# Attention with row sums in the output matmul: output blocks 130 PSUM columns apart in place of 129

## The chip, the cores and the metric

The kernel runs on one NeuronCore of a Trainium2 chip. The metric is device time in microseconds (us), from executions of the whole program. A time is the median of several runs. A profile is one more execution with every instruction recorded. On one core a run's state is "fast" unless it is over 1.5% above the fastest of its kernel.

## The reference, cut to what matters

```python
B, H, Sq, Sk, D = 16, 32, 192, 1024, 128          # bf16
scores = einsum("bhqd,bhkd->bhqk", q, k) * D ** -0.5
p = softmax(scores, axis=-1)
out = einsum("bhqk,bhkd->bhqd", p, v)
```

There are 512 heads, and the kernel takes them two at a time: 256 pairs of heads.

## The kernel before: the parts that matter here

For each head TensorE transposes the keys (`tr`), multiplies keys by queries (`qk`), and multiplies exponentials by values (`pv`). ScalarE computes the exponentials, VectorE copies the transposed keys to SBUF and normalises the output, POOL copies the values into rows that end in a one. That extra column makes the output matmul 129 columns wide: column 128 of the result is the row sum.

The 192 queries are three blocks j of 64. The two heads x of a pair use the two column halves of the array. So one key tile t of one block j is a *couple* of matmuls (x = 0 and 1) that run together, and a pair of heads needs 3 x 8 = 24 couples, issued as two halves of 12.

```python
VB = 130
vp = sb("f_vp", [128, R, 2 * T, VB], BF16)          # value rows: 128 values, ones; 260 bytes apart
o_ps = ps("f_o", [128, 512], F32)                   # one PSUM bank for the output of a pair
# ... TensorE:
order = [(j, t) for j in range(3) for t in range(T)]    # T = 8 key tiles

def pv(p, lo, hi):
    if lo == 0:
        take(s_vp, 1)
        # ...
        if 1 <= p <= NPR - 3:
            take(s_on, 1)                           # VectorE has read the pair before out of o_ps
    O = o_of(p)
    for j, t in order[lo:hi]:
        for x in range(2):
            ins = pe.matmul(
                O[64 * x: 64 * x + 64, j * 129: j * 129 + 129],
                pt[:, (2 * p + x) % NP, t * SQ + j * 64: t * SQ + j * 64 + 64],   # stationary
                vp[:, p % R, x * T + t, 0:129],                                   # moving
                start=t == 0, stop=t == T - 1, skip_group_check=True,
                tile_position=(0, 64 * x))
    # ...

def step(n):
    for x in range(2):
        h = 2 * n + x
        qk(h); tr(h + 2); pv(n - 2, 12 * x, 12 * x + 12)     # bounds left out
# steps run in a hardware loop of R = 4 steps per iteration
# ... VectorE, once a pair:
def onorm(p):
    O = o_of(p)[:, 0:387].rearrange("p (j c) -> p j c", j=3)
    ri = rinv[:, 3 * p: 3 * p + 3]
    dve.wait_ge(s_pv, p + 1)
    dve.reciprocal(ri, O[:, :, 128]).then_inc(s_rc, 1)
    dve.wait_ge(s_rc, p + 1)
    # ...
    dve.tensor_tensor(ob[:, so, a, :].rearrange("p (j d) -> p j d", j=3), O[:, :, 0:128],
                      ri.unsqueeze(2).to_broadcast([128, 3, D]), ALU.mult,
    ).then_inc(s_on if p < NPR - 1 else s_fin, 1)
```

Of the kernel before, what the change touches and what calls it, by code (L numbers as in the profile page):

```python
# [26 lines left out]
def _general_path(nc, q, k, v, out, redo, G=16, NS=2, LAGS=(2, 4, 5, 7), ROUTES=(R_W, R_W, R_EA)):  # L27
# [46 lines left out]
    with ExitStack() as es:  # L74
# [137 lines left out]
        def _(pe):  # L212
# [48 lines left out]
            def pv(u):  # L261
# [5 lines left out]
                if k3 == 0 and pr >= 2:  # L267
                    pe.wait_ge(s_on, pr - 1)
                O = o_ps[pr % 2]
                PTS = pt_sb[:, u % NPT]  # L270
# [5 lines left out]
                for t in range(KT_TILES):  # L276
                    first = t == 0
                    last = t == KT_TILES - 1
                    if k3 < 2:
                        x = a if k3 == 0 else b  # L280
                        ins = pe.matmul(O[:, sl, :], PTS[:, t, :], vs[:, s, x, t, :],
                                        start=first, stop=last, skip_group_check=True)
                        if with_rs:
                            ins = pe.matmul(O[:, 3, sl: sl + 1], PTS[:, t, :], ones[:, 0:1],
                                            start=False, stop=last, skip_group_check=True)
                    else:
                        pe.matmul(O[0:64, sl, :], PTS[:, t, 0:64], vs[:, s, a, t, :],
                                  start=first, stop=last, skip_group_check=True, tile_position=(0, 0))
                        ins = pe.matmul(O[64:128, sl, :], PTS[:, t, 64:128], vs[:, s, b, t, :],
                                        start=first, stop=last, skip_group_check=True, tile_position=(0, 64))  # L290
                        if with_rs:
                            pe.matmul(O[0:64, 3, sl: sl + 1], PTS[:, t, 0:64], ones[:, 0:1],
                                      start=False, stop=last, skip_group_check=True, tile_position=(0, 0))
# [108 lines left out]
def _attention_kernel(nc, q, k, v, out, NVS=6):  # L402
# [12 lines left out]
    VB = 130  # L415
# [10 lines left out]
    with ExitStack() as outer:  # L426
# [23 lines left out]
        with ExitStack() as es:  # L450
# [25 lines left out]
            def o_of(p):  # L476

                if p == NPR - 1:
                    return s_ps[0][:, 0:512]
                if p == NPR - 2:  # L480
                    return k_ps[:].bitcast(F32)
                return o_ps[:]
# [88 lines left out]
            def _(pe):  # L571

                def take(s, c):
                    pe.wait_ge(s, c).then_inc(s, -c)  # L574
# [42 lines left out]
# [3 lines that stand above are left out]
                        if p == NPR - 1:  # L620
                            take(s_exp, 2)
                        if 1 <= p <= NPR - 3:
                            take(s_on, 1)
                    O = o_of(p)
                    ins = None
                    for j, t in order[lo:hi]:
                        for x in range(2):
                            ins = pe.matmul(  # L628
                                O[64 * x: 64 * x + 64, j * 129: j * 129 + 129],
                                pt[:, (2 * p + x) % NP, t * SQ + j * 64: t * SQ + j * 64 + 64],  # L630
                                vp[:, p % R, x * T + t, 0:129],
                                start=t == 0, stop=t == T - 1, skip_group_check=True,
                                tile_position=(0, 64 * x))
                    if hi == len(order):
                        ins.then_inc(s_pv, 1)
# [4 lines that stand above are left out]
                        if h < NH:  # L640
                            qk(h)
                        if h + 2 < NH:
                            tr(h + 2)
                        if n >= 2:
                            pv(n - 2, 12 * x, 12 * x + 12)
# [22 lines left out]
            @block.vector  # L668
            def _(dve):
                def evac(h):  # L670
                    p, x = divmod(h, 2)
                    dve.wait_ge(s_tr, h + 1)
                    if p >= R:
                        dve.wait_ge(s_qk, h - 2 * R + 1)
                    dve.tensor_copy(  # L675
                        kt[:, p % R, 8 * x: 8 * x + 8, :],
                        k_ps[:].rearrange("d (t c) -> d t c", c=128),
                    ).then_inc(s_ev, 1)

                where = {}  # L680
                for i, (p0, c) in enumerate(stores):
                    for a in range(c):
                        where[p0 + a] = (i, a)

                def onorm(p):
                    i, a = where[p]
                    so = i % NSO
                    O = o_of(p)[:, 0:387].rearrange("p (j c) -> p j c", j=3)
                    ri = rinv[:, 3 * p: 3 * p + 3]
                    dve.wait_ge(s_pv, p + 1)  # L690
                    dve.reciprocal(ri, O[:, :, 128]).then_inc(s_rc, 1)  # L691
                    dve.wait_ge(s_rc, p + 1)
                    if a == 0 and i >= NSO:
                        dve.wait_ge(s_st[so], 16 * (i // NSO))
                    dve.tensor_tensor(  # L695
                        ob[:, so, a, :].rearrange("p (j d) -> p j d", j=3),
                        O[:, :, 0:128],
                        ri.unsqueeze(2).to_broadcast([128, 3, D]),
                        ALU.mult,
                    ).then_inc(s_on if p < NPR - 1 else s_fin, 1)  # L700

                cnt = [0]

                def check(lo, hi, i, part):
                    c = chk[:, lo:hi]
                    if part == 0:
                        ins = dve.tensor_scalar(c, rinv[:, lo:hi], 1.0 / RS_HI, 1.0 / RS_LO, ALU.max, ALU.min)  # L707
                    elif part == 1:
                        ins = dve.tensor_tensor(c, c, rinv[:, lo:hi], ALU.not_equal)  # L709
                    else:  # L710
                        ins = dve.tensor_reduce(bad[:, i: i + 1], c, mybir.AxisListType.X, ALU.max)  # L711
                    ins.then_inc(s_dv, 1)
                    cnt[0] += 1
                    dve.wait_ge(s_dv, cnt[0])

                evac(0)
                evac(1)
                for n in range(NPR + 2):
                    for x in range(2):
                        h = 2 * n + 2 + x  # L720
                        if h < NH:
                            evac(h)
                    if n >= 2:
                        onorm(n - 2)
                        if 0 <= n - 2 - EARLY < 3:
                            check(0, 3 * EARLY, 0, n - 2 - EARLY)
                for part in range(3):
                    check(3 * EARLY, 3 * NPR, 1, part)
                dve.sem_inc(s_fl, 1)  # L729
                dve.wait_ge(s_fl, 2)  # L730
                dve.tensor_copy(redo[0:1, 0:1], o_ps[0:1, 0:1]).then_inc(s_fl, 1)  # L731
                dve.wait_ge(s_fl, 3)
# [48 lines left out]
```

## Time and profile before

| | before |
|---|---|
| median of the first 3 runs | 978.72 us (978.32 to 980.33) |
| span of the profiled run, granted clock | 975.8 us, 0.994 |
| one pair of heads in the steady part (mean, from the trace's start times) | 3670.5 ns; times 256: 939.6 us |

These are lines of the page of the kernel before: the busy time of each engine with its share of the span, and three rows of the costliest groups. A group's row has line, engine, operation, output and inputs, shape, count; then busy us and mean ns of one; then the engine's idle time just before them.

```profile
PE 949.3 (97%) x30730; PEld 943.4 (97%) x30730; DVE 546.5 (56%) x1031; ACT 743.8 (76%) x513; POOL 267.5 (27%) x263
...
L628 PE MATMUL f_o<-f_vp,f_pt 128*64 128x129 bf16 x12192 | 455.1, 221 | 0.3 <-PEq L574 0.3
...
L695 DVE TENSOR_TENSOR f_ob<-f_o,f_rinv 128x384 bf16<-128x384 f32 x254 | 141.6, 558 | 9.0 <-DVE f_rinv L691 0.3
L691 DVE RECIPROCAL f_rinv<-f_o 128x3 f32<-128x3 f32 x254 | 46.0, 181 | 5.0 <-PE f_o L628 2.4
```

TensorE is the busy engine and the others have room. The view of waits says who waited for whom; here are its longest lines and TensorE's longest (total us, times, longest us).

```profile
POOL f_vp L565 <- PE f_o L628: 671.7, 251, 5.9
DVE f_kt L675 <- PE f_k L588: 404.2, 509, 6.1
ACT f_pt L740 <- PE f_s L609: 220.7, 509, 5.8
...
PE f_s L609 <- issue: 6.4, 4, 3.1
```

Everyone waits for TensorE and TensorE seems to wait for nobody. That isn't quite so. The Trainium skill, "Perfetto Trace Analysis", section "Tensor Engine Instruction (MATMUL, LD_WEIGHTS)", says that a matmul's recorded end is an estimate, while its start is a recorded event. So start times were compared. This is the timeline of one pair (start us, duration us, engine, line, operation, count):

```profile
401.87 0.90 PE L628 MATMUL f_o<-f_vp,f_pt 128*64 128x129 bf16 x24
...
402.57 0.86 PE L609 MATMUL f_s<-f_qt,f_kt 128*64 128x192 bf16 x20
402.80 0.18 DVE L691 RECIPROCAL f_rinv<-f_o 128x3 f32<-128x3 f32 x1
...
403.02 0.56 DVE L695 TENSOR_TENSOR f_ob<-f_o,f_rinv 128x384 bf16<-128x384 f32 x1
...
403.24 0.64 PE L588 MATMUL f_k<-f_ident,f_kn 128*64 128x128 bf16 x16
...
403.72 0.89 PE L628 MATMUL f_o<-f_vp,f_pt 128*64 128x129 bf16 x24
```

The second half of a pair's output matmuls starts at 401.87 and the next group at 402.57. Reciprocal and multiply follow and end at 403.58, and the next pair's output starts at 403.72. The transposes at 403.24 would have let it start about 0.03 us earlier, at 403.69. A gap that short hides under matmul records of 0.22 us, so the table of waits doesn't show it.

### The profile page before, as it was taken

The page shows a single profiled execution, that of the slowest core. Times are in us where ns is not written, and L with a number is a line of the kernel's source. Part 1 is how long each engine was busy: PE and PEld are TensorE (multiplying, and loading weights), DVE is VectorE, ACT ScalarE, POOL GpSimd, SP SyncE. Part 2 cuts the span into 40 slices and gives each one's busy share as a digit, 9 for nine tenths or more (in the row PEclk, how much of TensorE's full clock was granted, in tenths as well). Part 3 has the DMA queues.
Part 4 walks back from the last instruction along what each step waited for, and adds up shares of the span by engine and source line. Part 5 has one row for each costly group of instructions (what it writes and reads, how often), then busy time and mean ns, then how long its engine had stood idle before and what let it go on. Part 6 is the DMA issues. An engine that isn't in the chain of part 4 may idle for free. (4 is left out here: it accounts for less than half of the span.)

```text
span 975.8 us, 67645 instructions
## 1 busy us (share of the span) xinstructions
PE 949.3 (97%) x30730; PEld 943.4 (97%) x30730; DVE 546.5 (56%) x1031; ACT 743.8 (76%) x513; POOL 267.5 (27%) x263
## 2 busy tenths in 40 slices
PE   5899999999999999999999999999999999999996
PEld 4799999999999999999999999999999999999985
DVE  2355655555555555555556555555555555565563
ACT  4577777777777777777777777777777777777774
POOL 2222222222222222222222222222222222222220
PEclk9899999999999999999999999999999999999999
DMA  9899999999999999999999999999999999999991
GB/s 263 237 331 347 346 330 345 343 324 351 346 323 350 345 334 342 331 343 341 349 329 341 331 348 335 344 337 319 365 336 336 348 338 330 349 337 327 352 321 44
DMA packets 279631, 319.32 MB, mean 327 GB/s; under 512 B 115744, under 2 KB 148512, under 8 KB 279584
## 3 DMA queue, kind: packets, MB, share of 16 engines
q1 hardware_dynamic: 279584, 318.84, 103.1%
q14 instruction: 35, 0.29, 0.1%
q8 instruction: 12, 0.20, 0.1%
HBM read 268.44 MB, written 25.17 MB: 301 GB/s over the span
## 5 line engine op out<-in xcount | busy, mean ns | idle before, releaser
L740 ACT ACTIVATE f_pt<-f_s 128x1536 bf16<-128x1536 f32 x512 | 742.5, 1450 | 220.8 <-PE f_s L609 220.7
L675 DVE COPY f_kt<-f_k 128x1024 bf16<-128x1024 bf16 x512 | 354.1, 692 | 407.0 <-PE f_k L588 404.2
L565 POOL COPY f_vp<-f_vs 128x1024 uint32<-128x1024 uint32 x256 | 266.7, 1042 | 690.4 <-PE f_o L628 671.7
L628 PE MATMUL f_o<-f_vp,f_pt 128*64 128x129 bf16 x12192 | 455.1, 221 | 0.3 <-PEq L574 0.3
L609 PE MATMUL f_s<-f_qt,f_kt 128*64 128x192 bf16 (+2 forms) x10240 | 443.3, 231 | 10.9 <-issue 6.4
L628 PEld LDWEIGHTS f_o<-f_vp,f_pt 128*64 128x64 bf16 x12192 | 391.7, 110 | 0.6 <-issue 0.6
L609 PEld LDWEIGHTS f_s<-f_qt,f_kt 128*64 128x64 bf16 x10240 | 359.2, 110 | 11.9 <-issue 11.8
L588 PE MATMUL f_k<-f_ident,f_kn 128*64 128x128 bf16 x8192 | 329.2, 219 | 6.2 <-PEq L574 4.8
L588 PEld LDWEIGHTS f_k<-f_ident,f_kn 128*64 128x64 bf16 x8192 | 286.1, 110 | 8.8 <-issue 8.6
L695 DVE TENSOR_TENSOR f_ob<-f_o,f_rinv 128x384 bf16<-128x384 f32 x254 | 141.6, 558 | 9.0 <-DVE f_rinv L691 0.3
L691 DVE RECIPROCAL f_rinv<-f_o 128x3 f32<-128x3 f32 x254 | 46.0, 181 | 5.0 <-PE f_o L628 2.4
L650 PE MATMUL f_o<-f_ones 128*128 128x512 bf16 x8 | 3.6, 631 | 1.1 <-POOL f_ones L555 1.1
L650 PEld LDWEIGHTS f_o<-f_ones 128*128 128x128 bf16 x8 | 1.0, 141 | 2.7 <-issue 1.7
L740 ACT ACT_TABLE_LOAD x1 | 1.3, 1283 | 0.8 <-PEq L766 0.8
L628 PE MATMUL f_s<-f_vp,f_pt 128*64 128x129 bf16 x48 | 1.8, 220 | 0.1
L628 PEld LDWEIGHTS f_s<-f_vp,f_pt 128*64 128x64 bf16 x48 | 1.5, 110 | 0.2 <-issue 0.2
L665 PEld LDWEIGHTS f_o<-f_bad,f_ones 128*1 128x1 bf16 x1 | 0.1, 79 | 1.6 <-DVEq L729 1.6
L628 PE MATMUL f_k<-f_vp,f_pt 128*64 128x129 bf16 x48 | 1.6, 220 | 0.0
L665 PE MATMUL f_o<-f_bad,f_ones 128*1 128x1 bf16 x1 | 0.2, 164 | 1.4 <-DVEq L729 1.4
L628 PEld LDWEIGHTS f_k<-f_vp,f_pt 128*64 128x64 bf16 x48 | 1.5, 110 | 0.0
L709 DVE TENSOR_TENSOR f_chk<-f_chk,f_rinv 128x744 f32<-128x744 f32 (+1 forms) x2 | 1.4, 706 | 0.0
L711 DVE TENSOR_REDUCE f_bad<-f_chk 128x1 bf16<-128x744 f32 (+1 forms) x2 | 1.1, 550 | 0.0
(15 smaller groups left out, 4.0 us busy)
## 6 DMA issues: line engine op xcount, KB each, us to landing
f_vs<-in_v_dram SPq DMA_DIRECT2D x256, 512.0 KB, 4.9
f_kn<-in_k_dram SPq DMA_DIRECT2D x255, 512.0 KB, 5.8
out_dram<-f_ob SPq DMA_DIRECT2D x63, 384.0 KB, 5.0
f_qt<-in_q_dram SPq DMA_TRANSPOSE x256, 4.6
f_kn<-in_k_dram SPq DMA_DIRECT2D x2, 256.0 KB, 2.9
out_dram<-f_ob SPq DMA_DIRECT2D x1, 288.0 KB, 2.3
out_dram<-f_ob SPq DMA_DIRECT2D x1, 96.0 KB, 2.0
```

Source lines behind the costliest of these rows:

```text
L565: gp.tensor_copy(vp[:, p % R, :, 0:D].bitcast(U32), vs[:, p % NVS, :, :].rearrange("p x (t d) -> p (x t) d", d=D).bitcast(U32),).then_inc( ...
L588: ins = pe.transpose(k_ps[64 * z: 64 * z + 64, t * 128: t * 128 + 128], kn[:, p % R, x, c0: c0 + 64], ident[:], tile_position=(0, 64 * z))
L609: ins = pe.matmul(S[64 * w: 64 * w + 64, c0: c0 + (j1 - j0) * 64], kt[:, p % R, 8 * x + t, 64 * w: 64 * w + 64], mv, start=True, stop=True ...
L628: ins = pe.matmul(O[64 * x: 64 * x + 64, j * 129: j * 129 + 129], pt[:, (2 * p + x) % NP, t * SQ + j * 64: t * SQ + j * 64 + 64], vp[:, p ...
L650: pe.matmul(o_ps[:], ones[:], ones[:].unsqueeze(1).to_broadcast([128, 4, 128]), start=True, stop=True)
L665: pe.matmul(o_ps[0:1, 0:1], ones[:, 0:1], bad[:, 0:1], start=True, stop=False)
L675: dve.tensor_copy(kt[:, p % R, 8 * x: 8 * x + 8, :], k_ps[:].rearrange("d (t c) -> d t c", c=128),).then_inc(s_ev, 1)
L691: dve.reciprocal(ri, O[:, :, 128]).then_inc(s_rc, 1)
L695: dve.tensor_tensor(ob[:, so, a, :].rearrange("p (j d) -> p j d", j=3), O[:, :, 0:128], ri.unsqueeze(2).to_broadcast([128, 3, D]), ALU.mul ...
L709: ins = dve.tensor_tensor(c, c, rinv[:, lo:hi], ALU.not_equal)
L711: ins = dve.tensor_reduce(bad[:, i: i + 1], c, mybir.AxisListType.X, ALU.max)
L740: act.activation(pt[:, h % NP, :], s_ps[h % 2][:], ACT_FN.Exp, scale=scale).then_inc(s_exp, 1)
```

## The change

A PSUM column is 4 bytes here. Blocks at columns 0, 129, 258 begin at bytes 0, 516 and 1032: the middle one is not at a multiple of 8. At 0, 130, 260 all are. The Trainium skill, "PSUM — Partial Sum Buffer", Specifications, gives PSUM 8-byte cachelines, and the presumable intent was to start each block on such a line. No instruction, wait or byte is added or removed; the instruction streams of both kernels are otherwise the same.

```diff
-                                O[64 * x: 64 * x + 64, j * 129: j * 129 + 129],
+                                O[64 * x: 64 * x + 64, j * VB: j * VB + 129],
...
-                    O = o_of(p)[:, 0:387].rearrange("p (j c) -> p j c", j=3)
+                    O = o_of(p)[:, 0:3 * VB].rearrange("p (j c) -> p j c", j=3)
```

## The prediction

> **What bounds the kernel now.** The page's busy table has TensorE at 97% of the span of 975.8 us, ScalarE 76%, VectorE 56%, POOL 27%; the clock was 0.994. The table of waits has almost nothing on TensorE's side (under 20 us), while ScalarE waits 221 us and VectorE 404 us for it. From the start times of single matmuls in the trace (steady part), one pair of heads takes 3670.5 ns: two score blocks of 668, two transpose blocks of 447 and 473, two output blocks (12 pairs of matmuls each) of 702 and 713. 256 pairs make 939.6 us; the rest is start and end.
>
> **What the change touches.** Blocks j=0,1,2 of the output stood at columns 0, 129, 258, so at bytes 0, 516, 1032; now 0, 130, 260, so at bytes 0, 520, 1040. Only j=1 began off an 8-byte boundary. The Trainium skill, "PSUM — Partial Sum Buffer", Specifications, gives PSUM 8-byte cachelines; the presumable intent is to have every block start on one, for TensorE's writes and VectorE's reads. No instruction, wait, byte or column is added or removed.
>
> **TensorE's share.** Before already holds the comparison, since j=0 and j=2 are aligned and j=1 is not. Median distances between successive pairs of matmuls, for four key tiles: j=0 56, 59, 59, 59; j=1 56, 60, 59, 59 (first half) and 57, 61, 59, 59 (just after the transposes); j=2 56, 60, 59, 59. The misaligned block is no slower: its means for four are 234.5 and 236.1 against 235.0 (j=0) and 234.0 (j=2). Even if the whole 2 ns were alignment it would be about 0.5 us (estimate: 2 ns x 256). The 3 ns that three of four pairs pay follows the key tile, not j: it goes with the moving operand's rows, 260 bytes apart, which the change leaves alone.
>
> **VectorE's share.** The one consumer is the pair of reciprocal (181 ns) and multiply (558 ns, 384 elements; groups by form), and it is on the critical path: the first matmul of the next pair's output comes 148 ns after the multiply's end in practically every pair, 1179 ns after the last matmul of the previous one. In about three of four pairs this holds TensorE 34 ns beyond its usual 26 (in the others the loop's end delays TensorE by about 40 anyway). So a faster multiply would be worth up to 34 ns x 192 = 6.5 us, and a slower one costs fully. But I expect no change: three runs of 128 elements, none merged with the next in either layout; at most one more line touched in one run of three, about 1 ns of 558, so 0 to 0.3 us.
>
> **Predicted time.** 978.72 - 0.3 = 978.4 us, range 975.5 to 981.0 (runs of before alone spread over 2 us). Chances: faster by over 2% 0.01, within 2% 0.98, slower 0.01.
>
> **What would show it.** Right: the output matmuls' mean stays at 220 to 221 ns and the distances of j=1 as above; the multiply stays at 557 to 559 ns and reciprocal at 181; output blocks stay at 702 and 713 and the first output matmul stays 148 ns behind the multiply. Wrong: the multiply falls by 10 ns or more with the 60 ns gap before the output's first matmul shrinking; or the j=1 distances change; or the pattern over key tiles (56, 59, 59, 59) changes with the output's place.
>
> **What would make it wrong.** A penalty of misaligned PSUM rows hidden in VectorE's 558 ns, which I can't separate (before has no aligned variant of the multiply); or a write penalty that is spread over neighbouring blocks because the matmuls are pipelined, so that j=1's cost appears under all three. Both would make it faster, by under 1%. Slower I see only through an access that the wider stride makes dearer for VectorE.

## More of the kernel before

The output matmuls' mean of 221 ns is the length of one record; records overlap, so it isn't their rate. The group's busy time, 455.1 us, is the union of the records, and does follow the rate.

## The result, and the profile after

| | before | after |
|---|---|---|
| median us, same rounds (lowest to highest, 4 runs each) | 979.36 (978.32 to 980.33) | 978.27 (977.1 to 980.2) |
| ratio after / before | | 0.9996, 95% interval 0.998 to 1.0011 |
| profiled span us, granted clock | 975.8, 0.994 | 977.0, 0.992 |
| one pair, steady part, ns | 3670.5 | 3668.6 |

The ratio and its interval are from fast runs of the same rounds; the ratio is not the quotient of the medians quoted (0.9989), which lies in the interval too. The time is the same. The lines of the page of the kernel after that answer to those above:

```profile
PE 951.1 (97%) x30730; PEld 945.5 (97%) x30730; DVE 546.7 (56%) x1031; ACT 744.3 (76%) x513; POOL 268.5 (27%) x263
...
L628 PE MATMUL f_o<-f_vp,f_pt 128*64 128x129 bf16 x12192 | 455.5, 221 | 0.3 <-PEq L574 0.3
...
L695 DVE TENSOR_TENSOR f_ob<-f_o,f_rinv 128x384 bf16<-128x384 f32 x254 | 141.6, 558 | 9.0 <-DVE f_rinv L691 0.3
L691 DVE RECIPROCAL f_rinv<-f_o 128x3 f32<-128x3 f32 x254 | 46.0, 181 | 5.1 <-PE f_o L628 2.5
```

The output matmuls (455.5 against 455.1 us), the multiply (558 ns) and the reciprocal (181 ns) did not move. The timeline of the kernel after shows the same chain:

```profile
403.91 0.86 PE L609 MATMUL f_s<-f_qt,f_kt 128*64 128x192 bf16 x20
404.14 0.18 DVE L691 RECIPROCAL f_rinv<-f_o 128x3 f32<-128x3 f32 x1
...
404.36 0.56 DVE L695 TENSOR_TENSOR f_ob<-f_o,f_rinv 128x384 bf16<-128x384 f32 x1
...
405.06 0.89 PE L628 MATMUL f_o<-f_vp,f_pt 128*64 128x129 bf16 x24
```

The multiply ends at 404.92 and the output begins 0.14 us later, as before. From the start times of all steady pairs, the median distance between successive couples, in ns; the blocks j=1 and j=2 moved, and j=1 is the one that was off a multiple of 8 bytes:

```
                        j=0, t=0..7                    j=1, t=0..3      j=1, t=4..7      j=2, t=0..3
before                  56 59 59 59 56 59 59 59        56 60 59 59      57 61 59 59      56 60 59 59
after                   56 59 59 59 56 59 59 59        56 59 59 59      57 61 59 59      56 60 59 59
```

The one median that differs, 60 against 59, is no more than rounding: its mean went from 59.6 to 59.5 ns, and a mean in the block j=0, which did not move, from 59.6 to 59.3.

### The profile page after: what moved, and what is told of

The parts are those of the page before. It is cut to its first block, busy times and chain, and to the rows that moved or that the text cites. A ratio compares the mean times of both kernels' runs of the same rounds, so it can differ in the third digit from the quotient of the medians.

```text
span 977.0 us, 67645 instructions
## 1 busy us (share of the span) xinstructions
PE 951.1 (97%) x30730; PEld 945.5 (97%) x30730; DVE 546.7 (56%) x1031; ACT 744.3 (76%) x513; POOL 268.5 (27%) x263
## 5 line engine op out<-in xcount | busy, mean ns | idle before, releaser
L628 PE MATMUL f_o<-f_vp,f_pt 128*64 128x129 bf16 x12192 | 455.5, 221 | 0.3 <-PEq L574 0.3
```

Source lines behind the costliest of these rows:

```text
L628: ins = pe.matmul(O[64 * x: 64 * x + 64, j * VB: j * VB + 129], pt[:, (2 * p + x) % NP, t * SQ + j * 64: t * SQ + j * 64 + 64], vp[:, p % ...
```

## The experiments

Two questions were left. Is an odd start free, or was one odd block of three too little to see, or did VectorE hide it? And what are the 3 ns and the 34 ns, the two small losses that the prediction named as lying elsewhere? All experiments start from the kernel after, and are timed against the kernel before on the same chip (978.03 us in the rounds of the first four, 977.79 in those of the next three, 978.52 in those of the last two). On record the verdict on a difference under 2% is "same"; where smaller ones are read here, the reading rests on an interval that leaves out 1, and on start times.

### All three blocks at an odd column

```diff
-  O[64 * x: 64 * x + 64, j * VB: j * VB + 129],
+  O[64 * x: 64 * x + 64, 1 + j * VB: 1 + j * VB + 129],
...
-  O = o_of(p)[:, 0:3 * VB]...
+  O = o_of(p)[:, 1:1 + 3 * VB]...
```

> All three output blocks start on an odd column (1, 131, 261; 4 bytes past a multiple of 8), pitch 130; nothing else differs from the kernel after. Theory (a contiguous output's start does not matter to TensorE's writes nor to VectorE's reads): 978.3 us, within 0.3%; successive pairs of output matmuls stay 56, 59, 59, 59 apart in every block, the multiply stays at 557 to 559 ns. Rival 1 (there is a write penalty, but spread over neighbouring blocks by the pipeline, so that one odd block of three did not show it): three odd blocks triple it; output distances grow above 57/60 in every block. Rival 2 (VectorE pays for an odd row inside its 558 ns): the multiply grows by some ns per odd row, and the time by that times 256 because the multiply is on the critical path: 10 ns would be 2.6 us.

Measured: 978.18 us, ratio to before 0.9998 (0.9981 to 1.0014). The two groups in the view of groups by form:

```profile
L628 PE MATMUL f_o<-f_vp,f_pt 128*64 128x129 bf16 x12192 | 456.2, 221 | 0.3 <-PEq L574 0.3
...
L695 DVE TENSOR_TENSOR f_ob<-f_o,f_rinv 128x384 bf16<-128x384 f32 x254 | 141.6, 557 | 9.0 <-DVE f_rinv L691 0.2
```

Three odd blocks cost what none costs. The distances keep the pattern 56, 59, 59, 59, a half takes 701 ns as in the kernel after, and the multiply takes 557 ns. Both rivals fall.

### Interleaved blocks: a positive control

A result of "no difference" needs a test that could have shown one. Here block j lies in columns j, j+3, j+6, ...

```diff
-  O[64 * x: 64 * x + 64, j * VB: j * VB + 129],
+  O[64 * x: 64 * x + 64, j: j + 3 * 129: 3],
...
-  O = o_of(p)[:, 0:3 * VB].rearrange("p (j c) -> p j c", j=3)
+  O = o_of(p)[:, 0:387].rearrange("p (c j) -> p j c", j=3)
```

> Positive control: the three blocks are interleaved, block j at columns j, j+3, j+6, ..., so that every element of an output row lies in another 8-byte line than its neighbour; the same 387 columns, matmuls and reads. If TensorE's rate can be limited by the PSUM write at all, the distance of 56 to 59 ns between pairs of output matmuls must grow clearly (twice as many lines: up to 108 ns, which would be 24 x 50 ns x 256 = 300 us more), and if VectorE's read can be limited by lines, the multiply's 558 ns must grow. Theory: at least one of them grows, time over 1000 us, while odd starts cost nothing. Rival (writes and reads work element by element, whatever the lines): 978 us, distances and multiply unchanged; then alignment could not have mattered for that reason.

Measured: 1285.13 us, ratio 1.314 (1.3116 to 1.3164). In the groups by form:

```profile
L628 PE MATMUL f_o<-f_vp,f_pt 128*64 128x129 bf16 x12192 | 769.7, 311 | 0.3 <-PEq L574 0.3
...
L695 DVE TENSOR_TENSOR f_ob<-f_o,f_rinv 128x384 bf16<-128x384 f32 x254 | 141.6, 557 | 9.0 <-DVE f_rinv L691 0.3
```

The write can limit TensorE: the distance between couples goes to 110.0 ns in every block. (The first distance of a half is shorter, 66 or 69 ns.) Each of the 129 elements of a row now lies in another 8-byte line, so that is 110.0 / 129 = 0.85 ns a line. This agrees with the skill's Specifications on PSUM, whose line on cachelines says that non-contiguous patterns slow matmuls significantly. VectorE, reading with the same step, takes 557 ns: its read of three times 128 elements took no longer for it. So the change had nothing to win on VectorE's side.

### The 3 ns: value rows at 272 and at 264 bytes

The rows of the moving operand lie 260 bytes apart in SBUF. Only key tiles 0 and 4 start on a multiple of 16 bytes, and these are the ones that are followed by 56 ns in place of 59. The Trainium skill, "SBUF — State Buffer", Specifications, gives SBUF 16-byte cachelines.

```diff
   VB = 130
+  VR = 136                                  # 272 bytes; in the other run 132, 264 bytes
-  vp = sb("f_vp", [128, R, 2 * T, VB], BF16)
+  vp = sb("f_vp", [128, R, 2 * T, VR], BF16)
-  gp.memset(vp[:, :, :, D:VB], 1.0)
+  gp.memset(vp[:, :, :, D:VR], 1.0)
```

> The value operand's rows in SBUF get a pitch of 272 bytes (136 columns) in place of 260, so that every row starts on a multiple of 16 bytes; PSUM as in the kernel after. Theory (the 3 ns that three of four pairs of output matmuls pay come from moving rows that start off 16 bytes): all distances 56 ns, an output half 675 ns in place of 702, so 2 x 29 ns x 256 = about 14 us less: 964 us. Rival (they come from the weights' address, which also repeats every four key tiles modulo 512 bytes, or from the key tile's place in the accumulation): pattern 56, 59, 59, 59 and 978 us stay.

> The same with a pitch of 264 bytes (132 columns): even key tiles start on a multiple of 16 bytes, odd ones 8 bytes off. Theory (16 bytes count): distances 56, 59, 56, 59, a half about 690 ns, about 5 us less than the kernel after: 973 us. Rival (8 bytes suffice): all 56, as with 272 bytes: 964 us. Rival (the pattern has nothing to do with the moving rows): 56, 59, 59, 59 and 978 us.

Measured: 970.48 us with 272 bytes, ratio 0.9922 (0.9907 to 0.9936), and 973.06 us with 264, ratio 0.9946 (0.9932 to 0.9961). Median distances of the first half in ns, with the half's time:

```
260 bytes (after)   56 59 59 59 56 59 59 59 56 59 59 59     701
264 bytes           56 59 56 59 56 59 56 59 56 59 56 59     691
272 bytes           56 56 56 56 57 57 57 57 57 57 57 57     677
```

The pattern follows the rows' starts modulo 16, and 8 bytes don't suffice. The rival causes fall. So this loss has nothing to do with PSUM. The agreement with 16-byte lines goes as far as the start: a row of 258 bytes touches 17 such lines from each of the four starts, so it isn't the number of lines, and the runs don't show what it is. Nor is the 3 ns the net loss: with all rows at 272 bytes the distance is 57 ns and not 56, so a half of twelve couples lost 701 - 677 = 24 ns, 2 ns a couple.

With 272 bytes the time fell by 7.6 us and not by the 14 expected. The two halves did become shorter, by 23 and 24 ns a pair. But the half before the end of a loop iteration, one in four, did not: 733 ns in the kernel after and 764 ns now, where the ordinary one fell from 704 to 680 (why is read from the traces under "Why the prediction was right"). The pair's period fell by 32.8 ns (3668.6 to 3635.8); times 256 this is 8.4 us, near the measured gain. The expectation also took 56 ns for what is 57.

### The critical chain: the reciprocal twice

```diff
   dve.wait_ge(s_pv, p + 1)
+  dve.reciprocal(ri2[:], O[:, :, 128]).then_inc(s_r2, 1)
   dve.reciprocal(ri, O[:, :, 128]).then_inc(s_rc, 1)
```

> The kernel after with a second, unused reciprocal of the same three columns ahead of the real one. Theory (reciprocal and multiply stand on the critical path, so any cost of the new pitch for VectorE would have shown): the first output matmul of a pair comes 120 to 181 ns later after the previous pair's last one than the 1177 ns of the kernel after, and the time grows by as much times 256, 31 to 46 us, to 1009 to 1025 us. Rival (TensorE alone sets the pace and the constant 146 ns behind the multiply is chance): 978 us.

Measured: 993.83 us, ratio 1.0168 (1.0149 to 1.0186). The timeline:

```profile
401.96 0.86 PE L611 MATMUL f_s<-f_qt,f_kt 128*64 128x192 bf16 x20
402.19 0.18 DVE L693 RECIPROCAL f_ri<-f_o 128x3 f32<-128x3 f32 x1
...
402.29 0.15 DVE L694 RECIPROCAL f_rinv<-f_o 128x3 f32<-128x3 f32 x1
...
402.47 0.56 DVE L698 TENSOR_TENSOR f_ob<-f_o,f_rinv 128x384 bf16<-128x384 f32 x1
...
402.63 0.64 PE L590 MATMUL f_k<-f_ident,f_kn 128*64 128x128 bf16 x16
...
403.18 0.89 PE L630 MATMUL f_o<-f_vp,f_pt 128*64 128x129 bf16 x24
```

The size was mis-estimated: the second reciprocal starts 98 ns after the first and takes 150 ns, so the chain grew by 98 + 150 - 181 = 67 ns, not by 120 to 181. The mechanism holds. The first output matmul comes 1244 ns after the last one of the pair before (1177 in the kernel after), and 67 ns x 256 = 17.2 us stands against a measured 16.0 us over before. A VectorE cost of even 10 ns in this chain would have shown as 2.6 us.

### The critical chain made shorter, alone and together with the rows

VectorE copies the block out of PSUM (561 to 567 ns), frees the bank, and normalises from SBUF after the next copy of keys.

```diff
-  dve.reciprocal(ri, O[:, :, 128]).then_inc(s_rc, 1)
-  # ... multiply from O, which increments s_on
+  dve.tensor_copy(oc[:, :, 0:129], O[:, :, 0:129]).then_inc(s_cp, 1)
+  dve.wait_ge(s_cp, p + 1)
+  if p < NPR - 1: dve.sem_inc(s_on, 1)      # the bank is free
+  # in the next step, between the two copies of keys:
+  # reciprocal and multiply of the pair, reading oc in place of O
```

> The kernel after, but VectorE first copies the output block from PSUM to SBUF, releases the bank, and does reciprocal and multiply from SBUF one copy of keys later. Theory (VectorE's chain holds TensorE by 34 ns in three of four pairs): the gap before the first output matmul of a pair falls from 59 to 26 ns, time falls by up to 34 ns x 192 = 6.5 us to 972 us, unless the later copies of keys now hold TensorE. Rival (the wait is not the chain): 978 us or more.

> The copy first together with the value rows at a pitch of 272 bytes. If both gains are independent: 970.5 less 6.5 = about 964 us. If the time freed goes to the loop's end, as half of it did with 272 bytes alone (the output half before a loop's end was 780 ns in place of 680): 966 to 970 us.

Measured: 971.73 us for the copy alone, ratio 0.9936 (0.9923 to 0.995), and 962.83 us with both, ratio 0.9852 (0.9838 to 0.9865). Both are correct. The timeline of the copy alone:

```profile
402.59 0.86 PE L612 MATMUL f_s<-f_qt,f_kt 128*64 128x192 bf16 x20
...
402.90 0.56 DVE L693 COPY f_oc<-f_o 128x387 f32<-128x387 f32 x1
...
403.26 0.64 PE L591 MATMUL f_k<-f_ident,f_kn 128*64 128x128 bf16 x16
403.71 0.90 PE L631 MATMUL f_o<-f_vp,f_pt 128*64 128x129 bf16 x24
```

The copy ends at 403.46, well ahead of the output at 403.71, and the output now follows the transposes after 0.45 us in place of 0.48. The median gap before the first output matmul fell from 59 to 26 ns, and the time by 6.1 us against before in the same rounds, near the "up to 6.5 us" that the prediction had put on it. With both, the two gains add (6.1 and 7.6 us alone, 15.0 together): 962.83 us, 1.5% below before, is the fastest correct version. VectorE's busy time rose for it from 546.7 to 666.0 us.

### Does an odd start cost nothing, or does it cost nothing here?

The control showed that lines count, and the first experiment that the odd start doesn't. Counting resolves it. A row of 129 columns from byte 0 touches lines 0 to 64, which is 65 lines; from byte 4 it also touches 65. A row of 128 touches 64 from an even start and 65 from an odd one. So two kernels with 128-column matmuls were run. They give a wrong result: two value columns are overwritten by ones, and column 127 is the row sum.

```diff
-  gp.memset(vp[:, :, :, D:VB], 1.0)
+  gp.memset(vp[:, :, :, D - 2:VR], 1.0)     # VR = 136; POOL copies 126 values a row
-  vp[:, p % R, x * T + t, 0:129],
+  vp[:, p % R, x * T + t, 0:128],
-  dve.reciprocal(ri, O[:, :, 128])
+  dve.reciprocal(ri, O[:, :, 127])
-  O[64 * x: 64 * x + 64, j * VB: j * VB + 129],
+  O[64 * x: 64 * x + 64, j * VB: j * VB + 128],            # even
+  O[64 * x: 64 * x + 64, 1 + j * VB: 1 + j * VB + 128],    # odd, and O read from column 1
```

> Wrong result on purpose: output matmuls of 128 columns in place of 129 (the row sum takes the place of two value columns), value rows at 272 bytes, blocks at columns 0, 130, 260. It is the base of the odd variant. Every distance between pairs of output matmuls 56 ns (55.8 by 128 columns), time 965 to 971 us.

> The same, wrong on purpose, with the blocks at columns 1, 131, 261. A row of 129 columns touches 65 lines of 8 bytes from an even and from an odd start alike; a row of 128 touches 64 from an even and 65 from an odd start. Theory A (TensorE's write pays for each line touched, as the interleaved blocks showed at 110 ns for 129 lines): distances grow by one line, 0.8 ns, to about 56.8 ns (a half of twelve by 10 ns), and so would any row of an even number of columns. Theory B (a contiguous row costs nothing more from an odd start): distances as with the even start. Multiply unchanged in both.

Measured: 965.33 us from the even start (ratio 0.9867, 0.9844 to 0.989), 969.54 us from the odd one (ratio 0.9908, 0.9891 to 0.9926). The groups by form, first of the even, then of the odd start:

```profile
L629 PE MATMUL f_o<-f_vp,f_pt 128*64 128x128 bf16 x12192 | 440.4, 220 | 0.3 <-PEq L575 0.3
```

```profile
L629 PE MATMUL f_o<-f_vp,f_pt 128*64 128x128 bf16 x12192 | 445.0, 222 | 0.3 <-PEq L575 0.3
```

And the same group of the correct kernel with rows at 272 bytes, 129 columns from even starts:

```profile
L629 PE MATMUL f_o<-f_vp,f_pt 128*64 128x129 bf16 x12192 | 445.0, 221 | 0.3 <-PEq L575 0.3
```

An odd start of 128 columns costs 4.6 us of busy time. A half of twelve couples takes 676.8 ns against 667.6, so 9.2 / 12 = 0.77 ns a couple, about the 0.85 ns of one line from the control. The first two distances of the half show nearly nothing of it; from the fifth on the mean distance is 56.67 against 55.84 ns, 0.83 ns. It costs as much as the 129th column does from an even start (445.0 us both). Theory A holds. One rule fits the two widths and the interleaved rows at 0.77 to 0.85 ns a line: the distance goes by the 8-byte lines that a row touches, 65 for 129 columns wherever it starts. Where the moving rows lie 260 bytes apart, their 2 to 3 ns come on top. No other width was run.

## Why the prediction was right

- **TensorE.** It said that the unaligned block was no slower in the kernel before, so there was nothing to win. The distances after are the same, and three unaligned blocks cost nothing more. It read this off the distances and gave no cause. The cause shown afterwards is the count of lines: 65 from either start, because 129 is odd. That the width was odd is luck, as far as the prediction goes: it didn't count. An odd start is not free in general; with 128 columns it costs 0.77 ns a couple.
- **The 3 ns of three couples in four.** It put them on the moving rows, 260 bytes apart. That was right: rows at 272 bytes remove the pattern, and rows at 264 remove it for two more tiles in eight (2 and 6).
- **VectorE's time.** It allowed 1 ns for one more line, 0 to 0.3 us in all, without a measurement behind it. The multiply stayed at 558 ns, and takes 557 even with every element of a row in another line. No such term was found.
- **VectorE's place.** It said that reciprocal and multiply hold TensorE, that up to 6.5 us could be won there, and that a slower chain costs fully. Removing the hold gave 971.73 us against 977.79 for before in the same rounds, and 67 ns more cost 16 us. The constant distance behind the multiply was 146 ns after, not 148. It is 147 with all blocks unaligned, so this is not the alignment.
- **The loop's end.** It put about 40 ns on it; in the kernel before, the output half ahead of it took 740 ns against 704 for the others, so 36.
- **The time.** 978.4 us was said and 978.27 measured. That it is so close is chance: the runs of one kernel spread over 2 to 3 us, and the 0.3 us taken off for VectorE wasn't found.
- **Its own doubts.** A penalty hidden in the multiply's 558 ns, or one spread over neighbouring blocks, was named as what could prove it wrong. The interleaved and the all-odd kernel exclude both.

The loop's end was changed in no experiment, but the traces show much of it. The loop ends in a branch, the instruction that sends TensorE back to the loop's first step. These are its lines in the kernel before and in the kernel after (count; shortest, median and longest duration in ns; first and last start in us):

```profile
L658 PEldq COMPARE_BRANCH  x63: 83/215/4902, 19.5 to 941.7; - x63
L658 PEldq COMPARE_BRANCH  x63: 76/208/6298, 19.8 to 942.8; - x63
```

In the kernel after, the branch starts 210 ns after the last output half of the iteration does (medians), and the next group's first matmul 523 ns after the branch: 733 ns, as measured. In the runs with ordinary halves of 694 and 670 ns (rows at 264 bytes, 128 columns from an even start) these two figures are 209 and 524, and the half at the loop's end still takes 733. In the interleaved kernel, whose halves take 1279 ns, it takes no longer than the others. So what the runs show is a floor of about 733 ns and not an addition: shorter matmuls did not shorten that half. That the branch sets it is read from these constant distances; no run changed the loop. It also goes with the one figure that moved between before and after: the branch took 215 ns before, the next group started 532 ns after it, and the half took 740 ns. That is 7 ns in one pair of four, nearly the whole of 3670.5 - 3668.6 = 1.9 ns a pair. The all-odd kernel has 208 and 733 too, so this isn't the alignment.

What stays open: why a moving row that starts off 16 bytes costs 2 to 3 ns; why the branch is 7 ns shorter in all runs after the first kernel; and why, with rows at 272 bytes and with 128 columns from an odd start, about half of the loop ends are longer than 733 ns (medians 764 and 760), while with both edits they take 733 again.

## What to carry to other kernels

Before aligning an operand, count the lines that a row touches from the old and the new start: where the count is the same, as for the 129 columns here, there was nothing to win in these runs; with 128 columns an even start did win. If one of several blocks is already aligned, the profile of the kernel before holds the comparison; compare the distances between start times block by block, because durations and tables of waits don't show a few ns. And look at the other operand too: here it was the moving rows in SBUF, not the PSUM rows, that were worth aligning. Last, check an expected gain at the loop's end too: here a floor swallowed part of it.

## What the Trainium skill lacked or had wrong

- "PSUM — Partial Sum Buffer", Specifications, has the 8-byte cachelines, but not what a line costs or when a start matters. Here each touched line of an output row cost about 0.77 to 0.85 ns per couple of matmuls: 129 columns at a step of three took 110.0 ns, 128 contiguous columns from an odd start took 0.77 ns more than from an even one, and 129 contiguous columns took the same from both.
- That line speaks of matmuls only, and no page that was read here says that a VectorE read of PSUM doesn't depend on these lines: 384 fp32 elements took 557 to 558 ns at step one from even and odd starts and at step three.
- "SBUF — State Buffer", Specifications, asks for two hits on a 16-byte line. It doesn't say that a contiguous moving row that starts off 16 bytes delays the matmuls: here the next couple came after 59 ns, with starts 4, 8 and 12 bytes off alike, where it came after 57 with all rows on 16 bytes.
- No page has what the end of a hardware loop costs TensorE's stream of matmuls, beyond what a branch takes by itself. Here the branch took 208 ns and the next group started 523 ns after it began; the last group of an iteration took 733 ns where others took 704, 694 or 670, and no longer than the others where they took 1279.
